# Moving the X sums of a seven-product mixture of experts to VectorE and to other tiles, and ending its last group with eight products

## Chip, cores, metric

One core of one Trainium2 chip. The metric is device microseconds (us) of one execution, the median of several. Executions of one kernel agree within about 0.3%; every experiment was timed in five rounds together with the kernel before on the same chip.

## The reference

Eight attention-like batches give `x` (4608 tokens of 512 features). A gate and eight rounds of normalisation give P (4608 x 8), and eight dense experts follow.

```python
logits = x @ w_gate                       # x: 4608 x 512 from the attention part
P = np.exp(logits - logits.max())
for _ in range(8):                        # "routing" below
    P /= P.sum(1, keepdims=True) + 1e-09
    P /= P.sum(0, keepdims=True) + 1e-09
    P *= N / E
for e in range(8):
    h = np.maximum(x @ w1[e], 0.0)        # 512 -> 1024
    out += P[:, e:e + 1] * (h @ w2[e])    # 1024 -> 512
```

## The kernel before

Tokens are cut into nine groups of 512. Expert 0 runs as plain matmuls while the attention part and the routing still run. Experts 1 to 7 compute each 2 x 2 block product in seven block products instead of eight. This needs sums of quarters: of the weights (tiles T), of the hidden layer (tiles S), and of xT. The X sums are the same for all experts, so they are made once per group, stored in device memory (`Xd`) and loaded again for every expert.

The kernel plans itself. Every operation is recorded with its engine, an assumed duration, its dependencies and its tiles; a list scheduler then picks again and again the operation that could start first, and this fixes the order of instructions on every engine. A ring is a set of tiles that are handed out as they come free.

```python
ring("s_p", [128, 1024], BF16, "T", 9)
ring("s_p", [128, 4, 256], BF16, "S", 5)        # sums of the hidden layer: four per group
ring("s_p", [128, 2, 2, 256], BF16, "X", 3)     # sums of xT AND their later loads
# ... cut ...
def sums_x(g):
    X = [new("X") for _ in range(2)]
    # ... cut: x(n) is half n % 2 of tile n // 2
    for n, y, z, r in ((0, b12, b11, []), (1, b22, x(0), [0]), (2, b22, b12, []),
                       (3, b21, x(1), [1])):
        sub(dve if g < 6 else pool, 512, x(n), y, z, ALU.subtract, ...)
    for i in range(2):
        dma("SP", ..., nc.sync.dma_start(out=Xd[g][i], in_=X[i]()))

def load_x(g):
    X = [new("X") for _ in range(2)]
    for i in range(2):
        dma("SP", ..., nc.sync.dma_start(out=X[i](), in_=Xd[g][i]))
    return X
# ... cut, in the outputs of a group (down7) ...
    if e == 1:                                   # expert 0's outputs get their factor P
        for ts in range(4):
            act(512, lambda ts=ts: nc.scalar.activation(
                out=acc[g][:, ts, :], in_=acc[g][:, ts, :], func=ACT.Copy, bias=0.0,
                scale=P[:, 4 * g + ts, 0:1]), ...)
# ... cut, the main loop: the hidden layer of a group (un) is interleaved
# with the outputs of the group before (dn)
ORDER = "X1 x10 w10 x11 X2 x20 y10 x21 Z1 y11 X3 w11 x30 x31 x40 x41 w20 Y1 w21 X4 Z2".split()
for e in range(1, E):
    w1, w2 = load_w(e, ...)
    if e == 1:
        for g in range(NG):
            sums_x(g)
    A7, B7 = sums_w(e, w1, w2)
    for g in (list(range(NG)) if e < E - 1 else [8] + list(range(8))):
        X = load_x(g)
        hT = [new("hT") for _ in range(2)]
        un = up7(A7, g, X, hT, ["up0"])
        for n in ORDER:
            if len(n) == 3:
                un[n[:2], int(n[2])]()
            elif dn is not None:
                dn[n]()
        # ... cut ...
        dn = down7(e, g, hT, B7)
# the last group's outputs have no hidden layer to interleave with
for n in ORDER:
    if len(n) == 2:
        dn[n]()
dn["out"]()
```

## Time and profile before

| | before |
|---|---|
| median of runs | 1064.5 us (1063.76 to 1066.44) |
| profiled execution | span 1064.0 us, clock 0.996 |
| first seven-product matmul | 274.36 us |
| last group's first product to the end of the span | 1050.49 to 1064.0 us |

Engines: PE is TensorE, PEld its weight loads, DVE VectorE, ACT ScalarE, POOL GpSimd, SPq the queue from which stores and loads are issued. A line number in a profile line is that of the kernel that ran. Names in the lines: w are weights, hT the hidden layer, P_ with a number a bank of PSUM (the memory in which a product is summed up), U and V the copies that ScalarE makes of such banks, acc the outputs' sums. In the experiments' profiles the numbers are left out, so P is there either a bank or the routing's result.

First the busy view by windows of the kernel before. A row is a stretch in us from the span's start, its length, the busy us of each engine with the number of instructions, the granted TensorE clock, the DMA engines' share and GB/s.

```profile
core 0: us, PE busy (x) PEld busy (x) DVE busy (x) ACT busy (x) POOL busy (x), PEclk, DMA share, GB/s
228.00:274.36 46.36, 45.30 (x237) 21.36 (x240) 34.50 (x74) 21.25 (x38) 10.13 (x9) 0.96 0.32 86
274.36:300.00 25.64, 22.81 (x193) 18.45 (x191) 19.30 (x31) 25.25 (x49) 9.92 (x9) 1.00 0.43 92
300.00:320.00 20.00, 15.66 (x132) 13.06 (x131) 17.60 (x28) 9.94 (x22) 10.72 (x7) 0.94 0.35 121
320.00:340.40 20.40, 19.74 (x177) 17.32 (x175) 15.24 (x30) 13.06 (x27) 6.31 (x5) 0.97 0.22 72
340.40:1040.00 699.60, 699.60 (x6410) 626.84 (x6408) 538.64 (x963) 437.72 (x915) 300.93 (x239) 1.00 0.28 68
1050.40:1064.00 13.60, 6.86 (x59) 5.37 (x56) 7.30 (x13) 3.35 (x8) 5.70 (x5) 0.92 0.39 154
```

From 340 to 1040 us PE is never idle at full clock. A busy PE by itself is no proof of a good rate, so count its weight loads: 6408 in 699.6 us, one per 0.109 us, each with one 256-column matmul. This stretch has no slack. Time is lost only in the entry (131 weight loads in the 20 us from 300 to 320, where 183 fit) and in the tail. Two of the lines of the list of waits for 274 to 340 us say who was waited for (total, times, longest, us):

```profile
PE P_5744 L983 <- DVE S L896: 2.0, 1, 2.0
PE P_5553 L983 <- DVE S L896: 1.7, 1, 1.7
```

Next, PE's timeline in the kernel before around the first of these gaps (start, length in us, engine, line, operation, output and inputs):

```profile
297.35 0.60 PE L983 MATMUL P_5496<-xT,w_3831 128*128 128x256 bf16 x4
297.79 0.60 PE L983 MATMUL P_5503<-xT,w_3831 128*128 128x256 bf16 x4
298.22 1.03 PE L983 MATMUL P_5511<-w_3852,hT 128*128 128x256 bf16 x8
299.10 1.04 PE L983 MATMUL P_5544<-w_3852,hT 128*128 128x256 bf16 x8
301.85 1.05 PE L983 MATMUL P_5553<-w_3852,S 128*128 128x256 bf16 x8 [1.72 <-DVE S L896]
302.74 0.60 PE L983 MATMUL P_5565<-xT,w_3831 128*128 128x256 bf16 x4
303.17 0.60 PE L983 MATMUL P_5571<-X,w_3831 128*128 128x256 bf16 x4
```

Between the two products of plain xT quarters and the first product of X stand two products of hidden quarters and one of an S sum. It is the S product that waits. Why is no X product earlier in the order? The queue's timeline of the same kernel gives the stores of X sums (`xd_102<-X`) and their loads (`X<-xd_102`) of the group in question:

```profile
293.01 0.32 SPq L967 DMA_DIRECT2D xd_102<-X  x1
294.76 0.32 SPq L967 DMA_DIRECT2D xd_103<-X  x1
296.88 0.32 SPq L973 DMA_DIRECT2D X<-xd_102  x1
301.76 0.32 SPq L973 DMA_DIRECT2D X<-xd_103  x1
```

Its sums are stored and loaded again only moments before they are used.

PE's timeline of the tail of the kernel before:

```profile
1050.49 1.04 PE L983 MATMUL P_16324<-w_13344,hT 128*128 128x256 bf16 x8
1051.36 1.04 PE L983 MATMUL P_16348<-w_13344,hT 128*128 128x256 bf16 x8
1052.82 1.05 PE L983 MATMUL P_16357<-w_13344,S 128*128 128x256 bf16 x8 [0.42 <-DVE S L896]
1053.71 1.04 PE L983 MATMUL P_16348<-T,S 128*128 128x256 bf16 x8
1056.07 1.03 PE L983 MATMUL P_16348<-T,S 128*128 128x256 bf16 x8 [1.32 <-DVE acc_4739 L1087]
1056.94 1.04 PE L983 MATMUL P_16357<-w_13344,S 128*128 128x256 bf16 x8
1058.09 1.03 PE L983 MATMUL P_16348<-T,hT 128*128 128x256 bf16 x8
```

Seven products, with stalls between them: without a hidden layer to interleave with, the S sums and the reads of a bank that is added to later lie open.

### The profile page before, as it was taken

What the parts mean: (1) busy time and instruction counts of PE and PEld (TensorE: products, weight loads), DVE (VectorE), ACT (ScalarE), POOL (GpSimd) and SP (SyncE); (2) the same over time, 40 slices, a digit from 0 to 9 for tenths busy, and PEclk for the clock granted to TensorE, in tenths of its full rate; (3) what the DMA queues carried; (4) which work ended last, traced back from release to release, by engine and by line L of the source; (5) the groups of instructions that cost most, each with busy time, mean ns of one, the idle gap of its engine ahead of it and who ended that gap; (6) DMA issues with size and microseconds to landing.
All of it is one profiled execution on the core that took longest, in us unless ns stands there. A gap on an engine that the chain in (4) does not pass through costs nothing.

```text
span 1064.0 us, 24542 instructions
## 1 busy us (share of the span) xinstructions
PE 1021.8 (96%) x9498; PEld 842.4 (79%) x9536; DVE 834.4 (78%) x1628; ACT 711.4 (67%) x1568; POOL 496.8 (47%) x567
## 2 busy tenths in 40 slices
PE   6789999999989999999999999999999999999997
PEld 3456666654668888888888888888888888888886
DVE  6889989978697788877867887778777777787775
ACT  5799989944965666566666666666666665666664
POOL 8775756450163444443443443444443444334434
PEclk9999999999999999999999999999999999999999
DMA  9998986812531144113411251116111621114332
GB/s 144 152 179 136 136 143 120 139 41 70 90 130 60 41 90 87 44 41 80 90 41 48 53 110 50 41 50 120 41 41 41 114 57 50 41 42 128 121 118 119
DMA packets 104948, 91.57 MB, mean 86 GB/s; under 512 B 45312, under 2 KB 80256, under 8 KB 104832
## 3 DMA queue, kind: packets, MB, share of 16 engines
q1 hardware_dynamic: 64752, 63.78, 21.9%
q0 software_dynamic: 40080, 26.23, 18.3%
q8 instruction: 74, 1.21, 0.5%
q14 instruction: 42, 0.34, 0.1%
HBM read 94.98 MB, written 14.16 MB: 103 GB/s over the span
## 4 chain that ended last, share of the span: by engine, by line
PE 86%; DVE 5%; ACT 4%; issue 2%; POOL 2%; DMA 1%; ACTq 0%; DVEq 0%; POOLq 0%
DVE m L376 1%; DVE S L896 1%; DMA qk_r<-in_q_dram 1%; DVE xb L590 0%; DVE X L896 0%; ACT U L1011 0%; ACT V L1097 0%; POOL X L896 0%; PE P_6471 L983 0%; PE P_6315 L983 0%; PE P_5735 L983 0%; PE P_16154 L983 0%; PE P_12150 L983 0%; PE P_11799 L983 0%; PE P_8771 L983 0%
## 5 line engine op out<-in xcount | busy, mean ns | idle before, releaser
L983 PEld LDWEIGHTS <-S 128*128 128x128 bf16 x2016 | 197.1, 98 | 31.9 <-DVE S L896 5.9
L983 PEld LDWEIGHTS <-T 128*128 128x128 bf16 x1512 | 147.9, 98 | 19.4 <-issue 2.0
L983 PEld LDWEIGHTS <-hT 128*128 128x128 bf16 x1512 | 147.8, 98 | 18.4 <-DVE hT L1015 1.0
L896 DVE TENSOR_TENSOR S<-hT 128x1024 bf16<-128x1024 bf16 x126 | 85.8, 717 | 0.0
L1100 POOL TENSOR_TENSOR acc_4737<-acc_4737,V 128x512 f32<-128x512 f32 x28 | 35.8, 1284 | 54.7 <-ACT V L1097 54.3
L1100 POOL TENSOR_TENSOR acc_80<-acc_80,V 128x512 f32<-128x512 f32 x28 | 35.5, 1273 | 55.2 <-ACT V L1097 54.7
L1100 POOL TENSOR_TENSOR acc_79<-acc_79,V 128x512 f32<-128x512 f32 x28 | 37.3, 1337 | 51.1 <-ACT V L1097 50.6
L1100 POOL TENSOR_TENSOR acc_77<-acc_77,V 128x512 f32<-128x512 f32 x28 | 35.8, 1289 | 52.7 <-ACT V L1097 52.4
L1100 POOL TENSOR_TENSOR acc_4740<-acc_4740,V 128x512 f32<-128x512 f32 x28 | 35.8, 1288 | 49.5 <-ACT V L1097 49.4
L1100 POOL TENSOR_TENSOR acc_78<-acc_78,V 128x512 f32<-128x512 f32 x28 | 37.2, 1336 | 45.6 <-ACT V L1097 45.5
L1100 POOL TENSOR_TENSOR acc_4738<-acc_4738,V 128x512 f32<-128x512 f32 x28 | 35.6, 1276 | 46.0 <-ACT V L1097 45.4
L1100 POOL TENSOR_TENSOR acc_81<-acc_81,V 128x512 f32<-128x512 f32 x28 | 35.6, 1275 | 45.1 <-ACT V L1097 44.4
L1100 POOL TENSOR_TENSOR acc_4739<-acc_4739,V 128x512 f32<-128x512 f32 x28 | 35.7, 1283 | 43.8 <-ACT V L1097 43.3
L384 PEld LDWEIGHTS <-hT 128*128 128x128 bf16 x288 | 27.6, 100 | 23.5 <-issue 2.2
L896 DVE TENSOR_TENSOR S<-hT,S 128x1024 bf16<-128x1024 bf16 x63 | 46.0, 730 | 0.2
L896 DVE TENSOR_TENSOR S<-S,hT 128x1024 bf16<-128x1024 bf16 x63 | 44.1, 701 | 0.8
L384 PEld LDWEIGHTS <-w_449 128*128 128x128 bf16 x288 | 26.1, 99 | 23.4 <-issue 2.9
L384 PEld LDWEIGHTS <-qkT 128*128 128x128 bf16 x256 | 23.8, 100 | 20.7 <-DVE xb_r L595 4.4
L983 PEld LDWEIGHTS <-w_3831 128*128 128x128 bf16 x288 | 28.7, 99 | 5.1 <-issue 1.1
L983 PEld LDWEIGHTS <-w_5136 128*128 128x128 bf16 x288 | 28.2, 98 | 3.3
L983 PEld LDWEIGHTS <-w_13108 128*128 128x128 bf16 x288 | 28.2, 98 | 3.3
L983 PEld LDWEIGHTS <-w_11506 128*128 128x128 bf16 x288 | 28.2, 98 | 3.3
(4013 smaller groups left out, 3303.2 us busy)
## 6 DMA issues: line engine op xcount, KB each, us to landing
v_m<-in_v_dram SPq DMA_DIRECT2D x15, 512.0 KB, 4.6
qk<-in_k_dram POOLq DMA_DIRECT2D x15, 256.0 KB, 4.9
qk<-in_q_dram POOLq DMA_DIRECT2D x15, 256.0 KB, 5.7
X<-xd_98 SPq DMA_DIRECT2D x7, 256.0 KB, 2.6
X<-xd_99 SPq DMA_DIRECT2D x7, 256.0 KB, 2.7
X<-xd_100 SPq DMA_DIRECT2D x7, 256.0 KB, 2.6
X<-xd_101 SPq DMA_DIRECT2D x7, 256.0 KB, 2.7
X<-xd_102 SPq DMA_DIRECT2D x7, 256.0 KB, 2.6
```

Source lines behind the costliest of these rows:

```text
L376: dve(el, lambda: nc.vector.tensor_reduce(out=dst(), in_=src(), axis=AX.X, op=ALU.max, apply_absolute_value=True), r, w)
L384: nc.tensor.matmul(out_, lhsT=lhsT, rhs=rhs, start=start, stop=stop)
L896: lambda: f.tensor_tensor(out=out_(), in0=x(), in1=y(), op=op), r, w, **kw)
L983: pe(256, lambda i=i, k=k, z=z: nc.tensor.matmul(bank()[:, 256 * i:256 * i + 256], lhsT=lhs(k, i), rhs=rhs(k), start=first and z, stop=k = ...
L1100: pool(670, lambda: nc.gpsimd.tensor_tensor(out=acc[g][:, 2 * i:2 * i + 2, 256 * j:256 * j + 256], in0=acc[g][:, 2 * i:2 * i + 2, 256 * j: ...
```

## The change

Intent: (1) all X sums on VectorE, in S tiles, which are otherwise unused until the first outputs' sums; (2) the very last group's outputs in eight plain products, which need no S sums, each stored as soon as it is ready. For (2) the last expert must keep its second weight matrix intact, so its sum t1 goes to a T tile of its own. Cut are shapes that follow from the new tiles, a rewriting of expert 0's copies and of the sum t1 that computes the same, and variants that nine groups never reach (`g >= 9`, `e == 0`).

```diff
-        X = [new("X") for _ in range(2)]
+        X = [new("S") for _ in range(2)]
...
-            sub(dve if g < 6 else pool, 512, x(n), y, z, ALU.subtract,
+            sub(dve if g in (0,1,2,3,4,5,6,7,8) else pool, 512, x(n), y, z, ALU.subtract,
...
+        t1, t1k = q(w2, *b12), k(w2, *b12)
+        if 1 and e == E - 1:
+            T[0] = new("T")
+            t1, t1k = t(0), [T[0]]
...
+    def down8(e, g, hT, w2):
+        for ts in (2, 3, 0, 1):
+            py = new("P1")
+            for fc in range(8):
+                i, j = fc // 4, ts // 2
+                pe(512, lambda py=py, ts=ts, fc=fc: mm(
+                    py(), hT[fc // 4]()[:, fc % 4, ts * 128:ts * 128 + 128], w2()[:, fc, :],
+                    fc == 0, fc == 7), ...)
+            dve(580, lambda py=py, ts=ts: nc.vector.scalar_tensor_tensor(
+                out=acc[g][:, ts, :], in0=py(), scalar=P[:, 4 * g + ts, e:e + 1],
+                in1=acc[g][:, ts, :], op0=ALU.mult, op1=ALU.add), ...)
+            store(g, ts, 1)
...
-            dn = down7(e, g, hT, B7)
+            if 1 and e == E - 1 and g == 7:
+                down8(e, g, hT, w2)
+            else:
+                dn = down7(e, g, hT, B7)
```

More of the change, by code (lines that the diff above doesn't have):

```diff
@@ L682, in akey @@
     def akey(g):
-        return ["late"] if g >= NA else []
+        return ["late"] * (g >= NA) + ["P"] * (g >= 9)
     def up0(g, part):
@@ L694, in down0, with keys @@
         py = down(W[0][1], hts[g], tss, akey(g))
+        def keys(ts):
+            return [("acc", g, ts)] + [("acc", g, ts, j) for j in range(2) if g >= 9]
         for i, ts in enumerate(tss):
             if ts % 2:
-                act(512, lambda i=i, ts=ts: nc.scalar.copy(
-                    out=acc[g][:, ts, :], in_=py()[:, 512 * i:512 * i + 512]),
-                    [(py, i)] + akey(g), [("acc", g, ts)])
-            else:
-                dve(512, lambda i=i, ts=ts: nc.vector.tensor_copy(
-                    out=acc[g][:, ts, :], in_=py()[:, 512 * i:512 * i + 512]),
-                    [(py, i)] + akey(g), [("acc", g, ts)])
+                act(512, lambda i=i, ts=ts: nc.scalar.activation(
+                    out=acc[g][:, ts, :], in_=py()[:, 512 * i:512 * i + 512], func=ACT.Copy,
+                    bias=0.0, scale=P[:, 4 * g + ts, 0:1] if g >= 9 else 1.0),
+                    [(py, i)] + akey(g), keys(ts))
+            else:
+                dve(512, lambda i=i, ts=ts: nc.vector.tensor_scalar_mul(
+                    out=acc[g][:, ts, :], in0=py()[:, 512 * i:512 * i + 512],
+                    scalar1=P[:, 4 * g + ts, 0:1]) if g >= 9 else nc.vector.tensor_copy(
+                    out=acc[g][:, ts, :], in_=py()[:, 512 * i:512 * i + 512]),
+                    [(py, i)] + akey(g), keys(ts))
     halves, rests, W = {}, {}, {}
@@ L745, in expert0 @@
     def expert0(i):
-        if i < 0 or i >= 40:
+        if i < 0 or i >= (4 * (0 or NG) + 4):
             return
         plan.prio = 0
-        if i < 36:
+        if i < (4 * (0 or NG)):
             up0(i // 4, i % 4)
@@ L866, with store @@
         expert0(i)
-    def store(g, ts):
-        if g < 8:
+    def store(g, ts, one=0):
+        if one:
+            dma('SP', 1 << 18, 320, lambda: nc.sync.dma_start(
+                out=out[g * S:g * S + SM].rearrange('(p j) d -> p j d', j=NJ)[:, ts:ts + 1],
+                in_=acc[g][:, ts:ts + 1, :]),
+                [('acc', g, ts, j) for j in range(2)], [('out', g, ts)])
+        elif g < 8:
             if ts % 2:
@@ L898, in sums_w @@
     def sums_w(e, w1, w2):
+        eng = pool if e == 0 else dve
         def q(w, i, j):
@@ L905, in k @@
         def k(w, i, j):
-            return [(w, i, j)]
+            return [(w, i, j)] if e else [(w, n) for n in range(4)]
         S = [None] + [new("T") for _ in range(3)]
@@ L919, in sums_w @@
         late = ["late"] + (["P"] if e == 1 else [])
-        sub(dve, 1024, s(2), q(w1, *a11), q(w1, *a21), ALU.subtract,
+        sub(eng, 1024, s(2), q(w1, *a11), q(w1, *a21), ALU.subtract,
             k(w1, *a11) + k(w1, *a21) + late, [S[2]])
-        sub(dve, 1024, q(w1, *a21), q(w1, *a21), q(w1, *a22), ALU.add,
+        sub(eng, 1024, q(w1, *a21), q(w1, *a21), q(w1, *a22), ALU.add,
             k(w1, *a22) + late, k(w1, *a21))
-        sub(dve, 1024, s(1), q(w1, *a21), q(w1, *a11), ALU.subtract,
+        sub(eng, 1024, s(1), q(w1, *a21), q(w1, *a11), ALU.subtract,
             k(w1, *a21) + k(w1, *a11) + late, [S[1]])
-        sub(dve, 1024, s(3), q(w1, *a12), s(1), ALU.subtract,
+        sub(eng, 1024, s(3), q(w1, *a12), s(1), ALU.subtract,
             k(w1, *a12) + [S[1]] + late, [S[3]])
         b11, b12, b21, b22 = (0, 0), (0, 1), (1, 0), (1, 1)
-        sub(dve, 1024, t(2), q(w2, *b22), q(w2, *b12), ALU.subtract,
+        sub(eng, 1024, t(2), q(w2, *b22), q(w2, *b12), ALU.subtract,
             k(w2, *b22) + k(w2, *b12) + late, [T[2]])
-        sub(dve, 1024, q(w2, *b12), q(w2, *b12), q(w2, *b11), ALU.subtract,
-            k(w2, *b11) + late, k(w2, *b12))
-        sub(dve, 1024, t(1), q(w2, *b22), q(w2, *b12), ALU.subtract,
-            k(w2, *b22) + k(w2, *b12) + late, [T[1]])
-        sub(dve, 1024, t(3), q(w2, *b21), t(1), ALU.subtract,
+        t1, t1k = q(w2, *b12), k(w2, *b12)
+        if 1 and e == E - 1:
+            T[0] = new("T")
+            t1, t1k = t(0), [T[0]]
+        sub(eng, 1024, t1, q(w2, *b12), q(w2, *b11), ALU.subtract,
+            k(w2, *b11) + k(w2, *b12) + late, t1k)
+        sub(eng, 1024, t(1), q(w2, *b22), t1, ALU.subtract, k(w2, *b22) + t1k + late, [T[1]])
+        sub(eng, 1024, t(3), q(w2, *b21), t(1), ALU.subtract,
             k(w2, *b21) + [T[1]] + late, [T[3]])
@@ L940, in sums_w @@
         Bq = {"11": (q(w2, *b11), k(w2, *b11)), "21": (q(w2, *b21), k(w2, *b21)),
-              "22": (q(w2, *b22), k(w2, *b22)), "t1": (q(w2, *b12), k(w2, *b12)),
+              "22": (q(w2, *b22), k(w2, *b22)), "t1": (t1, t1k),
               "t2": (t(1), [T[1]]), "t3": (t(2), [T[2]]), "t4": (t(3), [T[3]])}
@@ L947, in xq @@
         return lambda: xT[:, 2 * i:2 * i + 2, 512 * g + 256 * j:512 * g + 256 * j + 256]
-    Xd = [[dram.tile([128, 2, 2, 256], BF16, name=f"xd{g}{i}") for i in range(2)]
+    Xd = [[dram.tile([128, 4, 256], BF16, name=f"xd{g}{i}") for i in range(2)]
           for g in range(NG)]
     def sums_x(g):
-        X = [new("X") for _ in range(2)]
+        X = [new("S") for _ in range(2)]
         def x(n):
-            return lambda: X[n // 2]()[:, n % 2]
+            return lambda: X[n // 2]()[:, n % 2 * 2:n % 2 * 2 + 2]
         b11, b12, b21, b22 = xq(g, 0, 1), xq(g, 0, 0), xq(g, 1, 1), xq(g, 1, 0)
@@ L972, in load_x @@
         for i in range(2):
-            dma("SP", 1 << 18, 250, lambda i=i: nc.sync.dma_start(out=X[i](), in_=Xd[g][i]),
+            dma("SP", 1 << 18, 250, lambda i=i: nc.sync.dma_start(out=X[i]().rearrange("p a b c -> p (a b) c"), in_=Xd[g][i]),
                 [("Xd", g, i)], [X[i], "order of X"])
@@ L1022, in relu @@
                 func=ACT.Relu, bias=0.0, scale=1.0), [x[fp]], [(hT[i], fp, j)])
-        more = [("banks", fp) for fp in range(2)]
+        more = [("banks", 0), ("banks", 1)]
         more += [k for n in ("s2", "s3", "22") for k in A[n][1]] + X + list(r0)
@@ L1039, in w1 @@
         def w1(fp):
-            prod(w, fp, "s1", "t1", True, A["s4"][1] + list(r0), hT, [("banks", fp)])
+            prod(w, fp, "s1", "t1", True, A["s4"][1] + r0, hT, [("banks", fp)])
         def x3(fp):
@@ L1057, in up7, with acc_part @@
             for fp in range(2)}
+    def acc_part(g, i, j):
+        return lambda: acc[g][:, 2 * i:2 * i + 2, 256 * j:256 * j + 256]
+    def down8(e, g, hT, w2):
[5 more added lines that the diff above has]
+                    py(), hT[fc // 4]()[:, fc % 4, ts * 128:ts * 128 + 128], w2()[:, fc, :],
+                    fc == 0, fc == 7), [(hT[i], fp, j) for i in range(2) for fp in range(2)]
+                    + [(w2, i, j) for i in range(2) for j in range(2)] + ["P"], [py])
+            dve(580, lambda py=py, ts=ts: nc.vector.scalar_tensor_tensor(
+                out=acc[g][:, ts, :], in0=py(), scalar=P[:, 4 * g + ts, e:e + 1],
+                in1=acc[g][:, ts, :], op0=ALU.mult, op1=ALU.add),
+                [py, "P"], [("acc", g, ts, j) for j in range(2)])
+            store(g, ts, 1)
     def down7(e, g, hT, B7):
@@ L1066, in hk @@
             return [(hT[j], fp, i) for fp in range(2)]
+        late, seen = akey(g), set()
         S = [new("S") for _ in range(4)]
@@ L1080, in prod, with start @@
             product(bank, lambda k, i: lhs()[:, k, 128 * i:128 * i + 128],
-                    lambda k: f()[:, k, :], 4, r + r2 + ["P"] + list(more), first)
+                    lambda k: f()[:, k, :], 4, r + r2 + (["P"] if e else late) + list(more), first)
+        def start(bank, i, j):
+            out_ = acc_part(g, i, j)
+            w = [("acc", g, 2 * i + n, j) for n in range(2)]
+            if (i, j) in seen:
+                dve(500, lambda: nc.vector.tensor_tensor(
+                    out=out_(), in0=bank().rearrange("p (a b) -> p a b", a=2), in1=out_(),
+                    op=ALU.add), [bank] + late, w)
+            else:
+                act(512, lambda: nc.scalar.copy(
+                    out=out_(), in_=bank().rearrange("p (a b) -> p a b", a=2)),
+                    [bank] + late, w)
+            seen.add((i, j))
         def read(bank, i, j):
+            if e == 0:
+                return start(bank, i, j)
             for n in range(2):
@@ L1093, in read2 @@
         def read2(bank, i, j):
+            if e == 0:
+                return start(bank, i, j)
             u = new("V")
@@ L1103, in read2 @@
                 [(u, 0), (u, 1)], [("acc", g, 2 * i + n, j) for n in range(2)])
-        if e == 1:
+        if e == 1 and g < 9:
             for ts in range(4):
@@ L1108, in down7 @@
                     out=acc[g][:, ts, :], in_=acc[g][:, ts, :], func=ACT.Copy, bias=0.0,
-                    scale=P[:, 4 * g + ts, 0:1]), ["P", ("acc", g, ts)],
+                    scale=P[:, 4 * g + ts, 0:1]), ["P", ("acc", g, ts)] + akey(g),
                     [("acc", g, ts, j) for j in range(2)])
@@ L1150 @@
     dn = None
-    for e in range(1, E):
-        w1, w2 = load_w(e, [("xT", 5, 3)])
-        if e == 1:
-            for g in range(NG):
+    for e in range(0 if 0 else 1, E):
+        w1, w2 = load_w(e, [("xT", 5, 3)]) if e else W[0]
+        if e == (0 if 0 else 1):
+            for g in (0,1,2,3,4,5,6,7,8):
                 sums_x(g)
         A7, B7 = sums_w(e, w1, w2)
-        for g in (list(range(NG)) if e < E - 1 else [8] + list(range(8))):
+        for g in (range(0, NG) if e == 0 else range(NG) if e < E - 1 else [8, *range(8)]):
             X = load_x(g)
@@ L1167 @@
                 dn["out"]()
-            dn = down7(e, g, hT, B7)
-    for n in ORDER:
-        if len(n) == 2:
-            dn[n]()
-    dn["out"]()
+            if 1 and e == E - 1 and g == 7:
+                down8(e, g, hT, w2)
+            else:
+                dn = down7(e, g, hT, B7)
+    if not 1:
+        for n in ORDER:
+            if len(n) == 2:
+                dn[n]()
+        dn["out"]()
     plan.run(tc)
```

## The prediction

> **What bounds it now.** TensorE. The busy view by windows gives PE 699.6 of 699.6 us from 340.4 to 1040 us at clock 1.00; a 256-column matmul takes 109 ns there. The change leaves that stretch alone. PE loses time in two places.
>
> 1. Entry into the seven-product experts, 274.4 to 340.4 us: some 500 matmuls at 109 ns are 55 us of work in 66 us; 11 are lost. Up to 300 us it is 4 us, with ScalarE busy 25.3 of 25.6 us (36 scalings of the outputs' sums by P, 0.61 us each, sit between the copies that PE waits for). From 300 to 320 us it is 5.6 us: by the list of waits PE waits 1.72 and 2.00 us for S tiles and 0.62 us for ScalarE; after that about 2 us run at half clock. The chain of waits runs through VectorE's X sums at 291.5 and 313.2: sixteen of them run from 291 to 334 us, because X has three buffers, shared by sums, stores and loads. Four GpSimd X sums (296.2 to 301.2) lie beside S sums that take 1.3 us instead of 0.68.
> 2. The tail, 1050.5 to 1064.0 us (timeline): 56 matmuls (6.1 us) end at 1059.1, after stalls of 0.4, 1.3 and 0.3 us (S sums; a bank read before it is added to); then two reads (0.9 us), a 512 KB store (2.7 us to landing) and the end.
>
> **What changes.**
> - All 36 X sums go to VectorE (0.33 us each) in S tiles, which are free until 284 us. I expect all of them between 228 and about 255 us, under the first expert's PE work. The sixteen late sums (5.4 us) leave the critical stretch: most of the 1.72, 2.00 and half-clock losses go. Gain about 5 us.
> - Against it: 28 more sums (9.3 us) fall into the routing's serial VectorE chain, which had some 9 us of gaps from 228 to 265 us and loses GpSimd's disturbance (its products took 1.45 and 0.88 us beside GpSimd's sums, 0.46 otherwise; the Trainium skill, GPSIMD Engine Reference, section Specifications, says GpSimd shares its SBUF interfaces with VectorE, in contention for instructions with two SBUF inputs, and these durations agree). I expect P 2 to 4 us later than 264.7. PE has first-expert work until 274.4, so it is mostly hidden, but the scaling slides with it: cost about 1.25 us.
> - The last group: 32 matmuls of 512 columns (216 ns each, estimated from two of 256: 6.9 us) for 56 of 256 (6.1 us), without stalls: PE ends near 1057.4; one read of 0.7 us; a last store of 256 KB (about 2.5 us). Gain 2.5 us.
> - A separate t1 tile for the last expert (seven of nine T buffers): 0 to 0.5 us. The rest of the diff is dead for nine groups.
>
> **Prediction.** Gain 5 - 1.25 + 2.5, about 6.5 us: 1058.0 us from 1064.5; 8 in 10 between 1053.5 and 1062.5. Over 2% faster 0.02, within 2% 0.97, over 2% slower 0.01.
>
> **What would show it.** X sums on VectorE only, done by about 255 us; P at 266 to 268 us; first seven-product matmul still at 274 to 276 us; no PE waits over 1 us for S from 299 to 317 us and full clock there; the steady rate unchanged; PE unbroken after the last hidden layer.
>
> **What would make it wrong.** The list scheduler putting sums ahead of each routing step, so that P comes over 5 us late and PE starves at 274 us; ScalarE's backlog alone keeping the stalls to 320 us (gain only 2 to 3 us); a reordering that costs waits in the steady stretch.

## More of the kernel before

What the planner expects to be late is ordered late.

## The result

| | before | after |
|---|---|---|
| median | 1064.51 us | 1055.17 us (1054.38 to 1056.06) |
| ratio, 95% interval | | 0.991 (0.9893 to 0.9927) |
| first seven-product matmul | 274.36 | 274.15 |
| from there to the last group's outputs | 776.1 us | 768.6 us |
| from there to the end of the span | 13.5 us | 11.25 us |

A ratio is the mean time of one kernel's fast runs over that of the other's fast runs in the same rounds, so it is not quite the ratio of the medians quoted.

The profiled executions differ by 10.0 us: 7.5 in the entry, 2.3 in the tail, 0.2 before. The last is noise: after's attention part happened to end 0.95 us later (at 228.63 against 227.68), although this code is the same.

The same windows of the changed kernel:

```profile
core 0: us, PE busy (x) PEld busy (x) DVE busy (x) ACT busy (x) POOL busy (x), PEclk, DMA share, GB/s
228.00:274.15 46.15, 45.75 (x246) 22.08 (x247) 40.16 (x104) 17.34 (x31) 0.81 (x1) 0.96 0.47 143
274.15:300.00 25.85, 22.76 (x202) 19.55 (x201) 19.41 (x33) 25.85 (x51) 5.89 (x5) 1.00 0.43 83
300.00:320.00 20.00, 19.92 (x182) 17.44 (x180) 12.90 (x24) 17.86 (x39) 9.13 (x8) 1.00 0.14 41
320.00:340.40 20.40, 20.40 (x190) 18.28 (x188) 15.89 (x30) 11.64 (x25) 7.75 (x7) 1.00 0.15 39
340.40:1035.00 694.60, 694.60 (x6365) 622.59 (x6363) 532.15 (x954) 436.22 (x909) 298.53 (x237) 1.00 0.28 70
1042.70:1054.00 11.30, 7.12 (x34) 3.08 (x32) 4.67 (x8) 0.00 (x0) 1.28 (x2) 0.96 0.48 186
```

Most of the loss from 300 us on is gone (180 weight loads in 20 us instead of 131); what remains lies nearly all before 300 us, where ScalarE is busy without a break. The only PE lines left in its list of waits for 274 to 340 us (PEld rows left aside) are two for ScalarE:

```profile
PE P_5278 L999 <- ACT U L1027: 1.8, 3, 0.8
PE P_5354 L999 <- ACT U L1027: 1.2, 1, 1.2
```

PE's timeline at the same point of the group that was shown for before:

```profile
296.48 0.60 PE L999 MATMUL P_5525<-xT,w_3831 128*128 128x256 bf16 x4
296.91 0.60 PE L999 MATMUL P_5532<-X,w_3831 128*128 128x256 bf16 x4
...
298.55 0.60 PE L999 MATMUL P_5525<-X,T 128*128 128x256 bf16 x4
...
302.27 1.04 PE L999 MATMUL P_5617<-w_3852,S 128*128 128x256 bf16 x8
```

The order has changed: products of X and xT fill the time until the S sums are ready. The loads (here by the queue) have gone ahead; those that before issued at 296.88 and 301.76 issue here at 282.88 and 288.91:

```profile
282.88 0.32 SPq L989 DMA_DIRECT2D X<-xd_102  x1
288.91 0.32 SPq L989 DMA_DIRECT2D X<-xd_103  x1
```

And the tail, four runs of eight 512-column matmuls without a break (PE's timeline of the changed kernel; the last read by VectorE takes 0.75 us, and a store of 256 KB 2.4 us to landing against 2.7 for 512 KB):

```profile
1042.75 1.89 PE L384 MATMUL P_16322<-w_13336,hT 128*128 128x512 bf16 x8
1044.48 1.89 PE L384 MATMUL P_16337<-w_13336,hT 128*128 128x512 bf16 x8
1046.21 1.89 PE L384 MATMUL P_16349<-w_13336,hT 128*128 128x512 bf16 x8
1047.93 1.89 PE L384 MATMUL P_16360<-w_13336,hT 128*128 128x512 bf16 x8
```

### The profile page after: what moved, and what is told of

Its sections match the earlier page's. It is cut to its first block, busy times and chain, and to the rows that moved or that the text cites. A ratio compares the mean times of both kernels' runs of the same rounds, so it can differ in the third digit from the quotient of the medians.

```text
span 1054.0 us, 24517 instructions
## 1 busy us (share of the span) xinstructions
PE 1022.4 (97%) x9512; PEld 841.3 (80%) x9512; DVE 824.6 (78%) x1634; ACT 707.8 (67%) x1560; POOL 475.4 (45%) x551
## 4 chain that ended last, share of the span: by engine, by line
PE 89%; ACT 4%; DVE 3%; DMA 2%; POOL 1%; issue 1%; DVEq 0%; ACTq 0%; POOLq 0%
DVE m L376 1%; DMA qkT<-qk 1%; ACT U L1027 1%; DMA qk_r<-in_q_dram 1%; DVE xb L590 0%; PE P_13550 L999 0%; PE P_12438 L999 0%; PE P_8591 L999 0%; PE P_15513 L999 0%; PE P_14556 L999 0%; PE P_14095 L999 0%; PE P_13743 L999 0%; PE P_13392 L999 0%; PE P_13188 L999 0%; PE P_12788 L999 0%
## 5 line engine op out<-in xcount | busy, mean ns | idle before, releaser
L999 PEld LDWEIGHTS <-S 128*128 128x128 bf16 x1984 | 194.1, 98 | 22.9 <-issue 0.5
L907 DVE TENSOR_TENSOR S<-hT 128x1024 bf16<-128x1024 bf16 x124 | 80.3, 684 | 0.0
L1155 POOL TENSOR_TENSOR acc_77<-acc_77,V 128x512 f32<-128x512 f32 x28 | 36.3, 1308 | 54.6 <-ACT V L1152 54.5
L1155 POOL TENSOR_TENSOR acc_78<-acc_78,V 128x512 f32<-128x512 f32 x28 | 37.4, 1349 | 49.0 <-ACT V L1152 48.9
L1155 POOL TENSOR_TENSOR acc_81<-acc_81,V 128x512 f32<-128x512 f32 x28 | 35.6, 1276 | 51.0 <-ACT V L1152 50.5
L1155 POOL TENSOR_TENSOR acc_4738<-acc_4738,V 128x512 f32<-128x512 f32 x28 | 35.5, 1274 | 51.1 <-ACT V L1152 50.5
L1155 POOL TENSOR_TENSOR acc_4740<-acc_4740,V 128x512 f32<-128x512 f32 x28 | 35.2, 1268 | 51.3 <-ACT V L1152 51.2
L1155 POOL TENSOR_TENSOR acc_80<-acc_80,V 128x512 f32<-128x512 f32 x28 | 35.4, 1269 | 49.9 <-ACT V L1152 49.3
L1155 POOL TENSOR_TENSOR acc_4737<-acc_4737,V 128x512 f32<-128x512 f32 x28 | 35.6, 1277 | 49.0 <-ACT V L1152 48.4
L1155 POOL TENSOR_TENSOR acc_79<-acc_79,V 128x512 f32<-128x512 f32 x28 | 35.8, 1289 | 48.1 <-ACT V L1152 47.6
L1155 POOL TENSOR_TENSOR acc_4739<-acc_4739,V 128x512 f32<-128x512 f32 x24 | 30.4, 1273 | 37.3 <-ACT V L1152 36.9
L907 DVE TENSOR_TENSOR S<-hT,S 128x1024 bf16<-128x1024 bf16 x62 | 42.3, 682 | 0.0
```

The lines of the kernel that those rows point to most:

```text
L907: lambda: f.tensor_tensor(out=out_(), in0=x(), in1=y(), op=op), r, w, **kw)
L999: pe(256, lambda i=i, k=k, z=z: nc.tensor.matmul(bank()[:, 256 * i:256 * i + 256], lhsT=lhs(k, i), rhs=rhs(k), start=first and z, stop=k = ...
L1155: pool(670, lambda: nc.gpsimd.tensor_tensor(out=acc[g][:, 2 * i:2 * i + 2, 256 * j:256 * j + 256], in0=acc[g][:, 2 * i:2 * i + 2, 256 * j: ...
```

## The experiments

Two theories of the entry's gain stood at first. **A**, that of the prediction: sixteen X sums cost VectorE's time between 291 and 334 us, and S sums came late behind them. **B**: GpSimd's X sums disturbed VectorE. After the second round a third was needed. **C**: with X shared, the sums of one group wait for the loads of another to be used up, so a group's sums, store and load follow one another late; with no X products to be had, the planner puts products there that depend on S sums and on reads of banks, and PE waits for those.

"Before" in a heading's ratio is the kernel before, in the same rounds.

### The tail alone

```diff
 # the changed kernel, with these lines as before
-        X = [new("S") for _ in range(2)]
+        X = [new("X") for _ in range(2)]
-            sub(dve if g in (0,1,2,3,4,5,6,7,8) else pool, 512, ...
+            sub(dve if g < 6 else pool, 512, ...
```

> Before plus the new last group alone (eight products, stores per 128 tokens, separate t1 tile for the last expert). By the two profiles the stretch from the last hidden products' end to the program's end shrank from 13.5 to 11.25 us: expected 2.0 to 2.5 us faster than before, entry stretch unchanged (PE waits of 1.7 and 2.0 us for S tiles still there). If the separate t1 tile costs anything at the start of the last expert, it shows as less than 2.0.

Measured: 1061.52 us against 1063.71; ratio 0.9977 (0.9963 to 0.9992), 2.4 us by the means. The waits for S in the entry are still there (4.0 us of PE). The tail is worth what its profile shows, and the separate t1 tile costs nothing that can be seen. Up to the first seven-product matmul its order on PE equals before's, and yet this took 45.1 us from the last transposes of the attention part, against 46.7 in before's profile: a difference of 1.5 us there need not come from an edit (the granted clock from 228 to 243 us was 1.00 here and 0.89 there).

### S tiles alone; VectorE alone; both

```diff
 # e2_s_tiles: before, with
-        X = [new("X") for _ in range(2)]      # in sums_x only
+        X = [new("S") for _ in range(2)]
 # e3_all_vector: before, with
-            sub(dve if g < 6 else pool, 512, ...
+            sub(dve, 512, ...
 # e4_sums_only: both
```

These kernels, like e1_tail_only, were built from the changed kernel with parts switched off, so they hold its rewritten copies; e3_all_vector, at before's time, shows no cost of those.

> Before, with the X sums in S tiles, but the engines as before (groups 0 to 5 on VectorE, 6 to 8 on GpSimd). Theory A (the loss was the sixteen sums that VectorE ran late, from 291 to 334 us, because X was shared with the loads): all sums finish before 265 us, the PE waits for S tiles after 299 us vanish, 5.5 to 8 us faster. Rival B (the loss was GpSimd's X sums disturbing VectorE[...]): GpSimd still makes its twelve sums, so at most half of the gain, under 4 us.

> Before, with all X sums on VectorE, but still in the three X tiles. Theory A: the sums stay late and there are more of them on VectorE after 285 us, so no gain in the entry stretch, 0 to 3 us slower there, less up to 1 us won in routing: within 2 us of before or slower. Rival B: GpSimd is gone from the sums, so most of the gain, 5 us or more faster.

> Both parts of the sums' change together, the tail as before. If tail and sums add up: 7 to 8 us faster than before (7.5 us entry by the profiles, about 1 us before it, less noise in the attention part), and with e1_tail_only's gain it sums to the whole change's 9.3 us.

| kernel | median (before 1063.71) | ratio, 95% interval | P after the last transposes | first seven-product matmul to PE's last |
|---|---|---|---|---|
| before (its profile) | | | 36.5 us | 784.8 us |
| e2_s_tiles | 1059.62 | 0.9957 (0.9944 to 0.9970) | 43.4 | 780.7 |
| e3_all_vector | 1063.37 | 0.9991 (0.9978 to 1.0004) | 31.8 | 785.4 |
| e4_sums_only | 1056.12 | 0.9922 (0.9910 to 0.9935) | 40.7 | 777.3 |

S tiles alone bring 4.6 us, less than A expected and more than B allowed; the engine alone brings nothing clear of noise. Together they bring 8.3 us, more than the sum: a new engine without new tiles is useless, and with new tiles it is worth 3.4 us of the last column. B as the cause in before is refuted by e3: it expected 5 us or more there. S sums of 1.64 us, against 0.68 at their shortest, are in e3's trace too, with no X sum on GpSimd; and that the four late sums which moved to VectorE cost what GpSimd's absence gained is not likely after e6_late_sums below, where sixteen cost 0.7 us. What GpSimd does in e2 is another thing: with free tiles its twelve sums run at once with VectorE's at 226 to 243 us, VectorE's X sums then take up to 1.37 us instead of 0.42 (GpSimd's 1.15 to 1.37), and P comes 43.4 us after the transposes. The Trainium skill, SBUF — State Buffer, section "Who interferes with whom", says that a VectorE instruction with two SBUF inputs contends with a GpSimd instruction that reads SBUF; these durations agree. In e2 ScalarE then has seven scalings in a row (its timeline) before the copy that PE waits for (PE's timeline):

```profile
270.94 4.39 ACT L1162 ACTIVATE acc<-acc,P 128x512 f32<-128x512 f32 x7
275.22 0.57 ACT L1027 COPY U<-P 128x512 f32<-128x512 f32 x1
```

```profile
275.84 1.01 PE L999 MATMUL P<-X,T 128*128 128x256 bf16 x4 [2.38 <-ACT U L1027]
```

The first matmuls after this gap lie 0.21 us apart, twice the usual; the granted clock was 0.50 from 276 to 279 us. In the tables "last transposes" is the start of the last group of transposes of the attention part, and P the start of the operation that writes P.

### The changed kernel again, and VectorE's time added back

```diff
 # e6_late_sums: the changed kernel, in the loop ahead of load_x, with plan.prio = -5000
+            if e == 1 and 2 <= g < 6:
+                for n in range(4):
+                    z = new("Z")                       # one scratch tile, never read
+                    sub(dve, 512, z, xq(g, n // 2, 0), xq(g, n // 2, 1), ALU.subtract,
+                        [hidden layer of group g - 2], [z])
```

> The changed kernel again, on the chip that also runs the next three, as their yardstick: 0.990 to 0.992 of before, first seven-product matmul 45 us after the attention part's last transposes, P 41 us after them, and about 3 us of PE waits for ScalarE's copies between 274 and 288 us.

> The changed kernel plus sixteen useless X-like sums (same shape, a scratch tile, no store) on VectorE, four after each hidden layer of groups 0 to 3 of the second expert, ahead of other VectorE work, about where before ran its late ones. Theory A (VectorE's time in the entry stretch was the loss): 3 to 6 us slower than the changed kernel, and PE waits for S tiles of 1 us and more are back between 285 and 325 us. Rival C (the loss was the order and the waits for buffers that sharing the three X tiles with the loads forced, not VectorE's time): within 1 us of the changed kernel.

Measured on one chip: the changed kernel 1054.46 us, ratio 0.9899 (0.9884 to 0.9914); with the sixteen sums 1055.13, ratio 0.9907 (0.9892 to 0.9923). Sixteen late sums on VectorE, wedged between the S sums, cost 0.7 us by the medians, and between 285 and 330 us PE waited for nothing. **Theory A falls**: VectorE's time was not what PE lacked. (This is shown in the changed kernel's order of instructions; the next run shows it in before.)

### One more X tile in the kernel before

```diff
-    ring("s_p", [128, 2, 2, 256], BF16, "X", 3)
+    ring("s_p", [128, 2, 2, 256], BF16, "X", 4)
```

> Before, with four X tiles instead of three and nothing else changed: the sums still share X with the loads, VectorE and GpSimd keep their groups. Theory C (the loss came from sums and loads waiting for one another's tiles, so that TensorE had no X products to run and the planner set S-dependent products in their place): 3 to 6 us faster than before, with the waits for S tiles of 1.7 and 2.0 us gone or under 1 us. Theory A (VectorE's time): the late sums remain on VectorE, so under 2 us.

Measured: 1058.9 us against 1065.33; ratio 0.9937 (0.9924 to 0.9951), 6.7 us by the means. This is before with one number changed. Sixteen of VectorE's X sums still run between 282 and 315 us, yet no wait of PE for an S tile is left: from 274 to 340 us PE waits only for ScalarE (2.2 us in all for its copies of hidden products, 1.3 for its reads of banks, none over 0.7). The first load of group 2 issues at 286.4 us instead of 296.9, those of group 3 by 293.3 instead of 310.4 and 315.7 (the queue's timeline), and products of X stand again before the S product (PE's timeline):

```profile
297.39 0.60 PE L983 MATMUL P<-X,w 128*128 128x256 bf16 x4
...
301.22 1.04 PE L983 MATMUL P<-w,S 128*128 128x256 bf16 x8
```

GpSimd keeps its twelve sums, but all of them now run before 247 us, where before ran four at 296 to 301; so this run is no test of B, and e3_all_vector is. In the profiles, from the first seven-product matmul to PE's last are 778.6 us (784.8 in before, 777.3 in e4_sums_only). So one more tile brings 6.2 of the 7.5 us. The Trainium skill, Perfetto Trace Analysis, section Optimization Strategy, says that consistent bubbles, the same gap again and again, can mean that there is not enough SBUF or PSUM for the next tile. Here the gaps were two of about 2 us, 14.4 us apart, and the run agrees, with one turn more: PE's wait named an S tile, not the X tile that was short.

### Late loads without shared tiles

```diff
 # e9_late_chain: the changed kernel, with the useless sums of e6_late_sums, but
+                        [first hidden quarter of group g - 1], [z])
+                dma("SP", ..., nc.sync.dma_start(out=Xz[g], in_=z()), [z], [("Xz", g)])
 # and in load_x of groups 2 to 5 of expert 1
-                [("Xd", g, i)], [X[i], "order of X"])
+                [("Xd", g, i), ("Xz", g)], [X[i], "order of X"])
```

> The changed kernel plus late useless sums as in e6_late_sums, but gated by the first hidden quarter of the group just before, stored to a scratch place, and the X loads of groups 2 to 5 made to wait for that store, so sums, store and loads follow one another as late as in before, with no tiles shared. Theory C: the loss of before returns, 3 to 6 us slower than the changed kernel, with X loads of these groups issued 5 us and more later than in e6_late_sums. If it was neither VectorE's time nor late loads but only waits for shared tiles: within 1 us of e6_late_sums.

Measured: 1065.38 us, ratio to before 0.9997 (0.9985 to 1.0010); the whole gain is gone, tail included, 10.4 us against the changed kernel by the ratios (0.9899 there, on another chip, 0.9997 here). That is more than the 3 to 6 us expected. The loads of groups 2 and 3 issue at 293.5 and 311.4 us, as late as before's 296.9 and 310.4; those of group 4 at 325.8 us are later than before's 316.3, so this run overshoots, and PE still loses time from 340 to 360 us (busy 18.24 of 20 us, where before is at 20.00). PE's timeline shows the pattern of before, now with another wait at its end:

```profile
295.32 1.04 PE L1002 MATMUL P<-xT,w 128*128 128x256 bf16 x8
296.19 1.91 PE L1002 MATMUL P<-w,hT 128*128 128x256 bf16 x16
297.94 1.04 PE L1002 MATMUL P<-w,S 128*128 128x256 bf16 x8
301.93 1.21 PE L1002 MATMUL P<-T,S 128*128 128x256 bf16 x8 [2.95 <-ACT V L1155]
302.93 1.06 PE L1002 MATMUL P<-xT,w 128*128 128x256 bf16 x4
303.78 1.06 PE L1002 MATMUL P<-X,w 128*128 128x256 bf16 x4
```

Products of the outputs stand where X products were, and PE waits 2.95 us for a read of a bank; after that a matmul takes 0.21 us (granted clock 0.50 from 303 to 306 us). With e6_late_sums and e8_four_x this shows C: late X loads are enough to bring a loss of this kind, without shared tiles, and VectorE's time is not. How much of the 10.4 us is the overshoot is not known. In no run does PE wait for the load itself; the lateness acts through the order that the planner makes of it. Whether early loads with before's order would still stall was not tried.

### P earlier

```diff
 # e7_sums_after_p: the changed kernel, with
+            for g in range(9):
+                sums_x(g, "S", ["P"] if g >= 4 else [])    # reads P: only after routing
```

> The changed kernel, with the X sums of groups 4 to 8 allowed only after P. The routing chain then meets 16 sums instead of 36, so P should come 4 to 6 us earlier (35 to 37 us after the last transposes). If a late P costs PE time through ScalarE's backlog as the prediction said (about 1.25 us), this is 0.5 to 2 us faster than the changed kernel; if the twenty sums between 262 and 285 us hurt as the late ones did, it is slower by 1 to 3 us.

Measured: 1056.92 us, ratio 0.9924 (0.9910 to 0.9937), 2.5 us slower than the changed kernel. P came 34.7 us after the transposes instead of 39.7 (the changed kernel in the same rounds), but now twenty sums, their stores and two loads of weights fall together in the stretch where ScalarE is full, and PE waits 3.8 us for ScalarE's copies (3.0 in the changed kernel), 0.5 for a read of a bank and 0.2 for hidden tiles. The first seven-product matmul, too, comes later, 45.3 us after the transposes instead of 44.1. The early sums are worth more than the early P. What a late P costs by itself is not isolated by this run.

### Less work for ScalarE, once and twice

```diff
 # e5_scale_vector: the changed kernel, expert 1's scaling of groups 4 to 8
-                act(512, lambda ts=ts: nc.scalar.activation(out=acc..., in_=acc..., scale=P...))
+                dve(260, lambda ts=ts: nc.vector.tensor_scalar_mul(out=acc..., in0=acc..., scalar1=P...))
 # e10_best: also, group 8's outputs take P as they are copied out of PSUM
-                    out=acc[g][:, ts, :], in_=py()[...], func=ACT.Copy, bias=0.0, scale=1.0)
+                    out=acc[g][:, ts, :], in_=py()[...], func=ACT.Copy, bias=0.0, scale=P[...])
```

> The changed kernel, with the scaling of the sums of groups 4 to 8 by P (20 of 36 operations) on VectorE instead of ScalarE. Theory: what is left of the entry's loss (about 4 us) is ScalarE's backlog of scalings, which starts with P. Then the PE waits for ScalarE's copies shrink and it is 1 to 3 us faster than the changed kernel. Rival: the scalings crowd VectorE as the late X sums did, waits for S or hidden tiles come back, and it is equal or slower.

> e5_scale_vector with one step more: group 8's first outputs are scaled by P as they are copied out of PSUM (their products end at about 275 us, after P), so its four scalings vanish from VectorE. ScalarE's and VectorE's work at 270 to 300 us falls by 1.3 us: 0 to 1 us faster than e5_scale_vector, 0.987 to 0.988 of before.

Measured: e5_scale_vector 1052.63 us (1052.19 to 1052.92), ratio 0.9882 (0.9867 to 0.9896), beside 1054.46 us (1054.06 to 1054.73) of the changed kernel on the same chip. It is 1.8 us faster than the changed kernel, and no run of the one overlaps with one of the other, so it beats both. PE's waits for ScalarE's copies fall from 3.0 to 1.6 us; 20 scalings of 0.476 us have found room on VectorE. The step after that brought nothing: 1054.47 us, ratio 0.9892 (0.9879 to 0.9906), on another chip than e5_scale_vector, an interval that overlaps with its own, and PE's waits for ScalarE were 2.1 us. My forecast of 0 to 1 us was a miss; the runs do not show why.

### The last stores in pairs

```diff
-            store(g, ts, 1)      # 256 KB after each product
+            store(g, ts)         # 512 KB after every second
```

> The changed kernel, with the last group's outputs stored two token tiles at a time (512 KB) instead of one (256 KB), the eight products as they are. If the tail's gain of 2.4 us comes from the products (no S sums, no stalls between them) and only a little from the smaller last store, this is 0.3 to 0.8 us slower than the changed kernel, 0.990 to 0.992 of before; if the store carried most of the gain, 1.5 us or more.

Measured: 1054.54 us, ratio 0.9897 (0.9882 to 0.9912); the changed kernel on another chip had 0.9899. I had expected 0.3 to 0.8 us slower; no difference can be seen in the times. In the profiles the end comes 4.6 us after PE's last matmul instead of 4.2. The tail's gain is the products'.

## Why the prediction was right, and where not

- **Total.** 1058.0 us predicted, 1055.17 measured, within the range (1053.5 to 1062.5), and a change of under 2% as said. The gain was 9.3 us, not 6.5. That the total came out right was in part luck: most of it rested on the entry, whose mechanism was wrong (below). The same edit to the tiles happened to remove the real cause as well.
- **What bounds the kernel, and where.** Right: the steady stretch keeps its rate (6363 weight loads in 694.6 us, 0.109 us each), and only entry and tail changed.
- **Entry, +5 and -1.25.** The term was too small (the 1.25 us for a late P was never measured by itself): 3.75 us net predicted, 7.5 measured in the stretch from the first seven-product matmul (e4_sums_only 777.3 against 784.8), 8.3 us by the timed means. And its mechanism failed, at the step "the sixteen late sums (5.4 us) leave the critical stretch: most of the 1.72, 2.00 and half-clock losses go". The losses went, but the sums' time had not made them: put back, the sums cost 0.7 us (e6_late_sums), while leaving them late and adding one tile won 6.7 us (e8_four_x). The prediction did name the shared X ring, as the reason for the sums being late, and did not ask what else is late because of it: the loads, and with them the X products that PE could have run.
- **GpSimd.** Its X sums beside the S sums looked guilty; taking them away alone did nothing (e3_all_vector). The runs show an effect of them only where the new tiles let them run during the routing (e2_s_tiles against e4_sums_only, 3.4 us in the entry).
- **P 2 to 4 us later, at 266 to 268 us.** Mis-sized: P is written by 270.2 us, 5.5 later than 264.7, because the planner set a sum between nearly all steps of the routing, and the sums ended at 260, not 255. Of the 5.5 us, 0.95 is the later end of the attention part; counted from the transposes P is 4.6 us later (41.1 against 36.5), and 3.2 in the other profile of the changed kernel (39.7). So the first of the listed ways to be wrong (over 5 us) was just met by the clock of the span and not by the change itself. PE did not starve: the first expert's products lasted until 274.1 us, and the first seven-product matmul came at 274.15.
- **Tail, 2.5.** Right: 2.4 us timed alone, 2.3 in the profiles; PE from first product to last 7.1 instead of 8.6 us, the rest 4.2 instead of 4.9. The smaller store was not needed for it.
- **Separate t1 tile, 0 to 0.5.** Nothing of it can be seen.

## What to carry to other kernels

When a wait names one tile, look at what else the waiting engine could have run and why that was not there: with a planned order, a shortage of tiles can show as a wait for something else. Before moving work to other engines or other buffers, try one more tile in the ring that two uses share; here one number gave 6.7 us, against 9.3 for the whole change. And test a suspected cost by adding it back to the fast version: a cause that costs 0.7 us there was not the cause of 7.

## What the Trainium skill lacked or had wrong

- Perfetto Trace Analysis, section Optimization Strategy: it has the shortage of tiles behind consistent bubbles, but says to find what the gap waits for. In this kernel, whose order is planned ahead, that wait named another tile than the one that was short: PE waited 1.7 and 2.0 us for S, and a fourth X tile removed both waits and 6.7 us.
- TensorE: Matmul & The Clock Gate, section "What's actually happening", gives the half clock after at least one idle window of about 3.4 us, free-running. Here shorter gaps were enough: single gaps of 2.38 us (e2_s_tiles) and 2.95 us (e9_late_chain) were followed by a granted clock of 0.50 and matmuls 0.21 us apart instead of 0.109. In before the 1.72 us gap ahead of 301.85 us was not; the 2.00 us gap ahead of 316.25 us was, from 318 to 321 us, but only after a further wait of 0.62 us. How much idle time within a window is enough, neither the section nor these runs say.
- VectorE: DVE Perf Modes times tensor_scalar at 2048 elements only. Scaling 128 x 512 FP32 in place by a scalar per partition took VectorE 0.476 us as profiled here, against 0.71 us and more on ScalarE.
